# First spectral input stage: the first tile's feature transform ahead of the second tile's transposes, the second tile's fold ahead of its moments, and six dummy matmuls fewer

## Chip, cores and metric

The kernel runs on one core of one Trainium2 chip. The metric is the device time of one execution in microseconds (us). Most executions of one kernel agree within 0.3%; here that is about 2 us.

## The reference

The model alternates two residual layers, twice. The change touches the first of them only.

```python
def _A_ref(x, w_r, w_i):                     # spectral mixer, x is 1 x 2048 x 576
    X = rfft2(x)                             # over tokens and features
    X = X * (w_r + 1j * w_i)
    return irfft2(X).astype(bfloat16)
x = x + _A_ref(_layernorm(x), w_r, w_i)      # layer 1: the stage studied is its input half
x = x + _B_ref(_layernorm(x), w1, b1, w2, b2)  # MLP 576 -> 4608 -> 576
# ... the same two once more
```

## The kernel before

The 2048 tokens are 16 tiles of 128 rows. In the first spectral input stage (0 to 33 us) each tile passes through

- VectorE: `fold` (sum and difference of the row's two halves), `half_moments` and `join_moments` (variance for the layer norm);
- TensorE: `turn` (five transposes into PSUM, which ScalarE copies to `xT`), then `dft_d` (the feature transform: six matmuls of 290 columns into PSUM);
- ScalarE: a copy `z` of that result, scaled by 1/sqrt(variance). Root and reciprocal are taken for two tiles at once, so tile 0's `z` waits for tile 1's moments;
- TensorE `dft_v`, and a copy `y1` by ScalarE or VectorE in turn, which a DMA then exchanges between partitions.

Tiles are counted below in the order of processing: tile 0, 1, 2, 3. `keep_busy(n)` issues n dummy matmuls of 512 columns, whose only purpose is to keep TensorE busy.

```python
def keep_busy(n, ps=None):
    pw = (ps or sm_ps)([P, 512], F32)         # takes one of the 2 small PSUM buffers
    for _ in range(n):
        nc.tensor.matmul(pw[:], lhsT=zeros[:], rhs=zeros[:, 0:1].to_broadcast([P, 512]), start=True, stop=True)

def turn(self, t):
    xf = self.st.pop(("xf", t))
    pt = sm_ps([P, 5, P])                     # the same 2 small buffers
    # ... five transposes, then the copy by ScalarE into xT

for i in range(NT + 4):                       # run_all, cut to what matters
    if 0 <= i - 1 < NT:
        (self.turn_halves if i == NT else self.turn)(order[i - 1])
    if i < NT:
        self.fold(order[i], nc.vector)
        if i == 0:
            half_moments(0)
    if i % 2 == 0 and 2 <= i <= NT:
        inverse(i // 2 - 1)                   # reciprocal for two tiles
    if i < NT:
        join_moments(i)                       # the aggregate
    # ... dft_v(order[i - 4])
    if 0 <= i - 2 < NT:
        (self.dft_d_halves if i - 2 == NT - 1 else self.dft_d)(order[i - 2])
    if i % 2 == 1 and i < NT:
        root(i // 2)                          # ScalarE, for two tiles
    if i < 4:
        keep_busy((5, 6, 1, 1)[i])
    if i + 1 < NT:
        half_moments(i + 1)                   # moments of the next tile, ahead of its fold
    # ... loads
```

Of the kernel before, what the change touches and what calls it, by code (L numbers as in the profile page):

```python
# [19 lines left out]
NT = 16  # L20
# [108 lines left out]
def kernel(  # L129
# [28 lines left out]
    def uid():  # L158
        _n[0] += 1
        return _n[0]  # L160

    def big_ps(shape, dtype=F32):
        return ps_big.tile(shape, dtype, tag="big", name=f"psb{uid()}")
# [39 lines left out]
    order = [t for q in QUADS for t in q]  # L203
# [13 lines left out]
    def keep_busy(n, ps=None):  # L217

        pw = (ps or sm_ps)([P, 512], F32)
        for _ in range(n):  # L220
            nc.tensor.matmul(pw[:], lhsT=zeros[:], rhs=zeros[:, 0:1].to_broadcast([P, 512]), start=True, stop=True)  # L221
# [95 lines left out]
    class SpectralIn:  # L317
# [102 lines left out]
            exchange(self.vx, t, y1)  # L420

        def dft_d(self, t):
            pz = big_ps([P, 2, 512])
            if ("xT2", t) in self.st:
                xT = self.st.pop(("xT2", t))
                for o in range(2):
                    at_rest = 4 * KH + o * KP
                    nc.tensor.matmul(pz[:, o, 0:KP], lhsT=xT[:, 4, :], rhs=c_fd2[:, at_rest : at_rest + KP], start=True, stop=False)
                    for part in range(2):
                        g = FOLDS.index((o, part))  # L430
                        nc.tensor.matmul(
                            pz[:, o, part * KH : (part + 1) * KH], lhsT=xT[:, g, :], rhs=c_fd2[:, g * KH : (g + 1) * KH],
                            start=False, stop=(part == 1),
                        )
            else:
                xT = self.st.pop(("xT", t))
                for o in range(2):
                    for q, ci in enumerate(HALF_CHUNKS[o]):
                        nc.tensor.matmul(
                            pz[:, o, 0:KP], lhsT=xT[:, ci, :], rhs=c_fd[:, 3 * o + q, :], start=(q == 0), stop=(q == 2),  # L440
                        )
            z = work.tile([P, 2, KP], BF16, tag="z", bufs=3)
            nc.scalar.activation(
                out=z[:].rearrange("p r (j o) -> p r j o", o=2),
                in_=pz[:, :, 0:KP].rearrange("p o (r j) -> p r j o", r=2),
                func=ACT.Copy, scale=self.st.pop(("rs", t)),
            )
            self.st["z", t] = z
# [17 lines left out]
        def run_all(self, loads):  # L466

            stats, moments, roots = {}, {}, {}

            def half_moments(n):  # L470
                stats[n] = work.tile([P, 2, nc.vector.BN_STATS_DIM], F32, tag="ln_stats", name=f"st{uid()}")
                for h in range(2):
                    nc.vector.bn_stats(out=stats[n][:, h, :], in_=x_sb[:, order[n], h * DH : (h + 1) * DH])

            def join_moments(n):
                if n % 2 == 0:
                    moments[n // 2] = work.tile([P, 2, nc.vector.BN_AGGR_DIM], F32, tag="ln_mv", bufs=4, name=f"mv{uid()}")
                nc.vector.bn_aggr(out=moments[n // 2][:, n % 2, :], in_=stats.pop(n)[:])

            def root(m):  # L480
                roots[m] = work.tile([P, 2], F32, tag="ln_v", name=f"sq{uid()}")
                nc.scalar.activation(out=roots[m][:], in_=moments.pop(m)[:, :, 1], func=ACT.Sqrt, bias=c_eps[:, 0:1], scale=1.0)

            def inverse(m):
                rs = work.tile([P, 2], F32, tag="ln_rs", bufs=4, name=f"rs{uid()}")
                nc.vector.reciprocal(out=rs[:], in_=roots.pop(m)[:])
                for i in range(2):
                    self.st["rs", order[2 * m + i]] = rs[:, i : i + 1]

            for i in range(NT + 4):  # L490
                if 0 <= i - 1 < NT:
                    (self.turn_halves if i == NT else self.turn)(order[i - 1])
                if i < NT:
                    self.fold(order[i], nc.vector)
                    if i == 0:
                        half_moments(0)
                if i % 2 == 0 and 2 <= i <= NT:
                    inverse(i // 2 - 1)
                if i < NT:
                    join_moments(i)  # L500
                if 0 <= i - 4 < NT - 1:
                    self.dft_v(order[i - 4], on_act=(i % 2 == 0 and i < NT))
                if i - 4 == NT - 1:
                    self.dft_v_halves(order[i - 4])
                if 0 <= i - 2 < NT:
                    (self.dft_d_halves if i - 2 == NT - 1 else self.dft_d)(order[i - 2])
                if i % 2 == 1 and i < NT:
                    root(i // 2)
                if i < 4:
                    keep_busy((5, 6, 1, 1)[i])  # L510
                if i + 1 < NT:
                    half_moments(i + 1)
                for call in loads.get(i, ()):
                    call()
# [427 lines left out]
    for n, (kind, j) in enumerate(early):  # L942
        i = 1 + 5 * n // 8
# [79 lines left out]
```

## Time and profile before

| | before |
|---|---|
| time, median of 3 runs | 743.07 us (742.95 to 743.47) |
| span of the profiled run | 740.7 us |
| landing of tile 1 of x (VectorE's wait for it ends) | 5.39 us |
| reciprocal for tiles 0 and 1 | 7.78 us |
| first `z` | 8.04 us |
| end of the stage (TensorE's next 16 dummies start) | 33.05 us |

From the page of the kernel before: the busy table (engine, busy us, share of the span, number of instructions) and, under it, the shares by engine of the chain of work that ended last.

```profile
PE 728.0 (98%) x5051; PEld 455.5 (61%) x5051; DVE 272.1 (37%) x937; ACT 309.2 (42%) x530; POOL 59.9 (8%) x117
...
PE 44%; ACT 1%; DVE 0%; issue 0%; ACTq 0%
```

The chain was followed back from the end to 403 us only, hence 44% for TensorE and next to nothing for the others. It doesn't reach the stage studied here.

TensorE looks saturated. The Trainium skill warns against this reading ("Trainium Kernel Development and Optimization", "Performance Expectations": "matmul busy time (the `TensorMatrix` row) is a bad metric for how close a kernel is to roofline"). In the stretch studied part of the busy time is dummies, so one has to look at what each engine waits for.

The timeline of TensorE in the kernel before: start in us, duration in us, engine, line, operation with output<-inputs, form and count; in brackets the idle time before it and what ended that.

```profile
1.00 2.31 PE L221 MATMUL pss_122<-zeros 128*128 128x512 bf16 x5 [1.00 <-DVE h_sb L240]
3.54 0.72 PE L353 MATMUL pss_131<-ident,xf 128*128 128x128 bf16 x5 [0.23 <-DVE xf L331]
4.06 2.58 PE L221 MATMUL pss_145<-zeros 128*128 128x512 bf16 x6
6.70 0.44 PE L353 MATMUL pss_157<-ident,xf 128*128 128x128 bf16 x5
6.97 0.91 PE L439 MATMUL psb_172<-c_fd,xT 128*128 128x290 bf16 x6
7.72 0.38 PE L221 MATMUL pss_181<-zeros 128*128 128x512 bf16 x1
7.94 0.44 PE L353 MATMUL pss_188<-ident,xf 128*128 128x128 bf16 x5
...
8.97 0.38 PE L221 MATMUL pss_211<-zeros 128*128 128x512 bf16 x1
9.42 0.44 PE L353 MATMUL pss_217<-ident,xf 128*128 128x128 bf16 x5
9.70 0.66 PE L455 MATMUL psb_232<-z,c_k_82 128*128 128x290 bf16 x4
...
33.05 3.64 PE L221 MATMUL pss_713<-zeros 128*128 128x512 bf16 x16 [0.24 <-ACT shared_113 L419]
```

Rows from L221 are the dummies: 5, 6, 1 and 1; the 16 at 33.05 mark the end of the stage. The six from 4.06 end only at 6.64, 0.43 us each; the row at 7.72 takes 0.22 until the next. A row with several matmuls gives their spacing: 6 transforms from 6.97 to 7.72 are 0.125 us apart. Tile 3's transposes start at 9.42.

The timeline of VectorE in the kernel before, from the landing of tile 1 on.

```profile
5.39 0.82 DVE L473 BATCH_NORM_STATS2 st_128<-x_sb 128x6 f32<-128x288 bf16 x2 [0.71 <-DMA x_sb<-in_A_x_dram]
6.12 0.29 DVE L331 TENSOR_TENSOR xf<-x_sb 128x288 bf16<-128x288 bf16 x1
...
6.55 0.21 DVE L478 BATCH_NORM_AGGREGATE mv_120<-st_128 128x2 f32<-128x12 f32 x1
...
7.78 0.16 DVE L486 RECIPROCAL rs_168<-sq_143 128x2 f32<-128x2 f32 x1
```

And of ScalarE in the same stretch.

```profile
6.79 0.30 ACT L482 ACTIVATE sq_143<-mv_120,c_eps 128x2 f32<-128x2 f32 x1 [0.50 <-DVE mv_120 L478]
7.17 0.69 ACT L355 COPY xT<-pss_157 128x640 bf16<-128x640 bf16 x1
8.04 0.74 ACT L443 ACTIVATE z<-psb_172,rs_168 128x580 bf16<-128x580 f32 x1 [0.18 <-DVE rs_168 L486]
8.68 0.69 ACT L355 COPY xT<-pss_188 128x640 bf16<-128x640 bf16 x1
```

The first `z` (8.04) was released by VectorE's reciprocal (7.78). That stands behind everything VectorE does from 5.39 on. Behind the `z` ScalarE copies tile 2's transposes (8.68 to 9.37), and tile 3's transposes, which need that PSUM buffer, start at 9.42.

### The profile page before, as it was taken

How to read it: one execution, taken by the hardware profiler on the slowest of the kernel's cores; microseconds unless marked ns; L12 is line 12 of the kernel's file. 1: busy time of each engine (PE TensorE's matmuls, PEld its weight loads, DVE VectorE, ACT ScalarE, POOL GpSimd, SP SyncE). 2: the span in 40 equal slices, each digit the busy share in tenths (PEclk: the TensorE clock that was granted, in tenths of full speed). 3: DMA queues.
4: the chain of work that ended last, by engine and by line, in shares of the span. 5: the costliest groups of instructions: out<-in, count | busy, mean ns of one | idle time of the engine just before them, and what ended most of it. 6: DMA issues, size and time to landing. Idle time of an engine off the chain costs nothing. (4 is left out here: it accounts for less than half of the span.)

```text
span 740.7 us, 12448 instructions
## 1 busy us (share of the span) xinstructions
PE 728.0 (98%) x5051; PEld 455.5 (61%) x5051; DVE 272.1 (37%) x937; ACT 309.2 (42%) x530; POOL 59.9 (8%) x117
## 2 busy tenths in 40 slices
PE   9989999999999999999998999999999999999997
PEld 6666644774487448744875575467547744774476
DVE  7895930555045604520355778011400140020011
ACT  7776856016511561156224686620361055005600
POOL 1230002002000200000003000110100010000000
PEclk9999999999999999999999999999999999999999
DMA  9577536212112102100117401450101010100000
GB/s 300 156 181 182 191 128 194 73 52 54 36 35 53 54 15 56 45 26 1 27 45 238 120 1 65 144 160 17 45 1 44 17 45 1 44 17 9 0 18 16
DMA packets 53097, 53.81 MB, mean 73 GB/s; under 512 B 30960, under 2 KB 44528, under 8 KB 53040
## 3 DMA queue, kind: packets, MB, share of 16 engines
q1 hardware_dynamic: 45232, 27.49, 13.6%
q0 software_dynamic: 7376, 24.96, 10.6%
q8 instruction: 39, 0.64, 0.4%
q10 hardware_dynamic: 432, 0.58, 0.2%
q14 instruction: 18, 0.15, 0.1%
HBM read 28.69 MB, written 8.59 MB: 50 GB/s over the span
## 5 line engine op out<-in xcount | busy, mean ns | idle before, releaser
L859 PEld LDWEIGHTS <-h_sb 128*128 128x128 bf16 x2304 | 224.9, 98 | 58.5 <-issue 1.0
L813 PEld LDWEIGHTS <-w_sb 128*128 128x128 bf16 x1152 | 109.4, 98 | 142.4 <-issue 17.2
L769 DVE TENSOR_SCALAR xn<-x_sb,mv,rs 128x576 bf16<-128x576 bf16 x24 | 9.4, 427 | 67.1 <-DMA quad_1809<-xn 28.8
L288 DVE BATCH_NORM_STATS2 stats<-x_sb 128x6 f32<-128x288 bf16 x78 | 30.9, 438 | 0.0
L821 PEld LDWEIGHTS <-w1r_sb 64*128 64x128 bf16 x288 | 10.8, 94 | 24.5 <-issue 16.9
L855 DVE TENSOR_TENSOR xb<-x_sb,b_bc 128x576 f32<-128x576 bf16 x32 | 24.0, 749 | 0.0
L569 PEld LDWEIGHTS <-h_sb 128*128 128x128 bf16 x128 | 12.1, 97 | 11.7 <-issue 5.2
L772 POOL COPY xn<-xn 128x64 bf16<-128x64 bf16 x24 | 6.4, 266 | 150.9 <-DVE xn L769 150.9
L221 PEld LDWEIGHTS <-zeros 128*128 128x128 bf16 x108 | 10.8, 102 | 11.5 <-issue 2.8
L827 ACT ACTIVATE h_sb<-psb_6037,b_sb 128x512 bf16<-128x512 f32 x2 | 1.3, 684 | 37.9 <-PE psb_6037 L821 37.9
L827 ACT ACTIVATE h_sb<-psb_6635,b_sb 128x512 bf16<-128x512 f32 x2 | 1.3, 684 | 37.8 <-PE psb_6635 L821 37.8
L827 ACT ACTIVATE h_sb<-psb_7233,b_sb 128x512 bf16<-128x512 f32 x2 | 1.3, 684 | 37.8 <-PE psb_7233 L821 37.8
L538 PEld LDWEIGHTS <-c_f_83 128*128 128x128 bf16 x128 | 12.3, 97 | 7.6 <-issue 3.0
L882 DVE TENSOR_TENSOR x_sb<-psb_7473,xb 128x576 bf16<-128x576 f32 x1 | 0.8, 758 | 43.4 <-PE psb_7473 L859 43.4
L882 DVE TENSOR_TENSOR x_sb<-psb_4089,xb 128x576 bf16<-128x576 f32 x1 | 0.8, 758 | 39.5 <-PE psb_4089 L859 39.5
L369 DVE TENSOR_TENSOR xf<-ef 128x256 bf16<-128x256 f32 (+1 forms) x56 | 13.6, 306 | 0.5
L882 DVE TENSOR_TENSOR x_sb<-psb_6875,xb 128x576 bf16<-128x576 f32 x1 | 0.8, 759 | 33.6 <-PE psb_6875 L859 33.6
L882 DVE TENSOR_TENSOR x_sb<-psb_6277,xb 128x576 bf16<-128x576 f32 x1 | 0.8, 758 | 33.6 <-PE psb_6277 L859 33.6
L455 PEld LDWEIGHTS <-c_k_82 128*128 128x128 bf16 x120 | 11.2, 98 | 2.5
L882 DVE TENSOR_TENSOR x_sb<-psb_3285,xb 128x576 bf16<-128x576 f32 x1 | 0.8, 757 | 28.8 <-PE psb_3285 L859 28.8
L882 DVE TENSOR_TENSOR x_sb<-psb_2483,xb 128x576 bf16<-128x576 f32 x1 | 0.8, 758 | 28.7 <-PE psb_2483 L859 28.7
L727 ACT ACTIVATE h_sb<-x_sb 128x576 bf16<-128x576 bf16 x16 | 11.2, 699 | 0.1
(1397 smaller groups left out, 1522.9 us busy)
## 6 DMA issues: line engine op xcount, KB each, us to landing
w_sb<-in_B_w_dram SPq DMA_DIRECT2D x16, 288.0 KB
v_sb<-in_B_w_dram POOLq DMA_DIRECT2D x4, 1152.0 KB, 6.0
shared_1504<-in_B_w_dram POOLq DMA_DIRECT2D x2, 1440.0 KB, 7.5
shared_5434<-in_B_w_dram POOLq DMA_DIRECT2D x2, 1440.0 KB, 7.5
v_sb<-shared_4685 SPq DMA_DIRECT2D x16, 145.0 KB
out_dram<-x_sb SPq DMA_DIRECT2D x15, 144.0 KB
v_sb<-shared_113 POOLq DMA_DIRECT2D x13, 145.0 KB, 3.4
b_sb<-shared_712 POOLq DMA_DIRECT2D x13, 145.0 KB, 6.6
```

Source lines behind the costliest of these rows:

```text
L221: nc.tensor.matmul(pw[:], lhsT=zeros[:], rhs=zeros[:, 0:1].to_broadcast([P, 512]), start=True, stop=True)
L288: nc.vector.bn_stats(out=stats[:, h, :], in_=x_sb[:, t, h * DH : (h + 1) * DH])
L369: nc.vector.tensor_tensor(out=xf[:, at0 : at0 + 2 * n].rearrange("p (g d) -> p g d", g=2), in0=ef[:, :, first : first + n], in1=ef[:, :, b ...
L455: nc.tensor.matmul(py[:, r, 0:KP], lhsT=c_k1[:, pl, :], rhs=z[:, ri], start=(q == 0), stop=(q == 1))
L538: nc.tensor.matmul(px[:, o, 0:KP], lhsT=c_f2[:, n // 4, pl, n % 4, :], rhs=vx[:, e, ri, :], start=(q == 0), stop=(q == 1))
L569: nc.tensor.matmul((ph, odd)[o][:, o, 0:KP], lhsT=i1[:, pl, n % 4, :], rhs=xp[:, ri, :], start=(q == 0), stop=(q == 1))
L727: nc.scalar.activation(out=at(h_sb, [P, D], 512 * 34), in_=x_sb[:, self.quad[i], :], func=(ACT.Copy, ACT.Square)[k], accum_out=self.s12[:, ...
L769: nc.vector.tensor_scalar(out=xn[:, 0:D], in0=x_sb[:, self.quad[i], :], scalar1=mean, scalar2=rs, op0=ALU.subtract, op1=ALU.mult)
L813: nc.tensor.matmul(acc[p][q], lhsT=w1_sb[:, ci, fc * 128 : (fc + 1) * 128], rhs=yT[:, ci, :], start=(first and ci == 0), stop=(not first a ...
L821: nc.tensor.matmul(acc[p][q], lhsT=w1r_sb[rows, p, :], rhs=yT[rows, 4, :], start=first, stop=not first)
L855: nc.vector.tensor_tensor(out=xb[:], in0=xr, in1=b2_bc[:].rearrange("p (h n) -> p h n", h=2), op=ALU.add)
L859: nc.tensor.matmul(po[:, h, 0:DH], lhsT=hts[fc][:, i * 128 : (i + 1) * 128], rhs=w2_chunk(fc)[:, h * DH : (h + 1) * DH], start=(fc == 0), ...
```

## The change

The intent is to fill TensorE's early time with real work instead of dummies. The transform of tile 0 goes ahead of tile 1's transposes, split from its scaled copy, which cannot run yet; six of the 13 dummies go; and tile 1's fold goes ahead of its moments, so that its transposes are fed sooner.

```diff
         def dft_d(self, t):
+            self.dft_d_sum(t)
+            self.dft_d_copy(t)
+
+        def dft_d_sum(self, t):
             pz = big_ps([P, 2, 512])
+            self.st["pz", t] = pz
# ... the matmuls
+        def dft_d_copy(self, t):
+            pz = self.st.pop(("pz", t))
# ... the scaled copy z
                     self.fold(order[i], nc.vector)
-                    if i == 0:
-                        half_moments(0)
+                    if i < 2:
+                        half_moments(i)
# ...
-                if 0 <= i - 2 < NT:
-                    (self.dft_d_halves if i - 2 == NT - 1 else self.dft_d)(order[i - 2])
+                if i == 1:
+                    keep_busy(2)
+                    self.dft_d_sum(order[0])
+                elif 0 <= i - 2 < NT:
+                    (self.dft_d_copy if i == 2 else self.dft_d_halves if i - 2 == NT - 1 else self.dft_d)(order[i - 2])
                 if i % 2 == 1 and i < NT:
                     root(i // 2)
-                if i < 4:
-                    keep_busy((5, 6, 1, 1)[i])
-                if i + 1 < NT:
+                if i == 0:
+                    keep_busy(5)
+                if 2 <= i + 1 < NT:
                     half_moments(i + 1)
```

## The prediction

> **What bounds the kernel.** TensorE is busy 98% of the 740.7 us span (busy table); the chain that ended last is nearly all TensorE. The change touches only the first 10 us of the first spectral stage (0 to 33 us). There the timeline shows TensorE running 13 dummy matmuls (5 from 1.00, 6 from 4.06, 1 at 7.72, 1 at 8.97). VectorE's chain sets the start: the second tile of x lands at 5.39 us (a 0.71 us wait for the DMA), then moments 5.39, fold 6.12, aggregate 6.55, moments and fold of tile 2, reciprocal 7.78; that releases ScalarE's first scaled copy z at 8.04. From 9.42 to 17 us TensorE is packed (1.52 us a tile); from 12.6 to 28 us VectorE is packed (3.18 us per two tiles). So the stage's end follows VectorE's early chain and the transposes of tile 3.
>
> **What the change does.**
> - Removes 6 of 13 dummies; nothing waits for them.
> - Tile 1's fold is ready about 0.73 us earlier (its moments move behind it), near 5.9. Its transposes queue behind the feature transform of tile 0.
> - That transform moves from 6.97 to about 5.1-5.6: it needs the first xT (copied by 4.99) and the transform constants, whose queue moves its last packets at 5.0 to 5.6. It probably runs at the slow clock. The Trainium skill ("TensorE: Matmul & The Clock Gate", Part 1) gives N/1.2 ns per matmul cold; the early dummies agree (0.43 us apart). Estimate for 6 matmuls of 290 columns: 1.45 us instead of 0.75, ending near 6.6-7.0. Tile 1's transposes then end near 6.9-7.5, against 7.14.
> - VectorE does the same work before the same reciprocal, but the aggregate now directly follows its own moments, which costs about 0.12 us (moments to aggregate is 0.85 for tile 0; with the fold between, 0.73 + 0.42).
> - z of tile 0 still waits for root and reciprocal, so it starts at 8.05 to 8.2; the advanced transform's result just waits in PSUM. The expected gain is off the critical path.
> - With fewer dummy tiles the small PSUM buffers alternate sooner. Before, tile 3's transposes (9.42) waited for the copy of tile 2 (ending 9.37) in their buffer, though the fold was ready at 9.15. Now they follow the fold, about 9.35: 0.06 us back, and 0.2 us of VectorE slack at 11.7 absorbs its 0.12.
>
> **Critical path.** Stage: about -0.1 to +0.15 us; later stages shift with it. The risk is the clock: TensorE gets gaps near 4.9-5.4, 7.0-7.9 and 8.9-9.3 that dummies filled. The same part of the skill says the array turns fast after a busy window of about 3.4 us, whose phase is free-running. In before it is fast from 6.70. If it turns later, tiles 1 to 3 run at half speed and 0.5 to 2 us are lost; about one chance in six.
>
> **Predicted time: 743.0 us, range 742.3 to 744.2.** Faster by over 2%: 0.3%; within 2%: 99%; slower: 0.7%.
>
> **What would show it.** Right: first z at 8.05-8.2, just behind the reciprocal; transform of tile 0 at 5.1-5.6, matmuls about 0.24 us apart; stage end (last y1 copies, 33.4 before) within 0.2 us; the rest shifted equally. Wrong: first z before 7.9, the stage's end moved by over 0.4 us, or the transform of tile 1 still slow (1.45 us, not 0.75).
>
> **What would make it wrong.** A later change to the fast clock; constants landing after 5.8 us, which would hold tile 1's transposes behind the waiting transform; a different landing of x; or load and exchange traffic shifting the 0.5 us wait for exchanged data at 37.2 us.

## The result

The changed kernel took 743.50 us (median of 6 runs, 742.36 to 743.84); the kernel before took 743.01 us in the rounds counted with it (6 runs, 742.67 to 743.50). The ratio is 1.0002, with a 95% interval of 0.9989 to 1.0015. A ratio is the mean time of one kernel's runs over that of the other's of the same rounds, so it is not quite the ratio of the medians.

From the page of the changed kernel, the busy table:

```profile
PE 726.3 (98%) x5045; PEld 454.5 (61%) x5045; DVE 272.1 (37%) x937; ACT 308.8 (42%) x530; POOL 59.9 (8%) x117
```

TensorE does 1.7 us less (728.0 to 726.3) and the span is 740.9 instead of 740.7: the busy time that went was worth nothing.

The timeline of TensorE in the changed kernel:

```profile
3.58 0.72 PE L353 MATMUL pss_128<-ident,xf 128*128 128x128 bf16 x5 [0.26 <-DVE xf L331]
4.09 1.06 PE L221 MATMUL pss_143<-zeros 128*128 128x512 bf16 x2
5.46 0.91 PE L444 MATMUL psb_146<-c_fd,xT 128*128 128x290 bf16 x6 [0.31 <-DMA c_fd<-const_fd]
6.21 0.44 PE L353 MATMUL pss_160<-ident,xf 128*128 128x128 bf16 x5
8.11 0.56 PE L353 MATMUL pss_182<-ident,xf 128*128 128x128 bf16 x5 [1.46 <-DVE xf L331]
...
9.40 0.56 PE L353 MATMUL pss_209<-ident,xf 128*128 128x128 bf16 x5
9.79 0.66 PE L463 MATMUL psb_224<-z,c_k_82 128*128 128x290 bf16 x4
...
33.18 3.64 PE L221 MATMUL pss_705<-zeros 128*128 128x512 bf16 x16 [0.24 <-ACT shared_113 L419]
```

The transform of tile 0 now runs at 5.46 instead of 6.97 (after a wait of 0.31 for its constants), tile 1's transposes at 6.21 instead of 6.70. Then TensorE waits 1.46 us for the fold of tile 2. Tile 3's transposes start at 9.40, nearly where they did before (9.42).

The timeline of VectorE in the changed kernel:

```profile
5.65 0.31 DVE L331 TENSOR_TENSOR xf<-x_sb 128x288 bf16<-128x288 bf16 x1 [0.94 <-DMA x_sb<-in_A_x_dram]
...
6.10 0.81 DVE L481 BATCH_NORM_STATS2 st_139<-x_sb 128x6 f32<-128x288 bf16 x2
6.95 0.21 DVE L486 BATCH_NORM_AGGREGATE mv_120<-st_139 128x2 f32<-128x12 f32 x1
...
8.18 0.16 DVE L494 RECIPROCAL rs_171<-sq_153 128x2 f32<-128x2 f32 x1
...
9.05 0.29 DVE L331 TENSOR_TENSOR xf<-x_sb 128x288 bf16<-128x288 bf16 x1
```

And of ScalarE:

```profile
7.19 0.29 ACT L490 ACTIVATE sq_153<-mv_120,c_eps 128x2 f32<-128x2 f32 x1 [0.86 <-DVE mv_120 L486]
...
8.38 0.74 ACT L451 ACTIVATE z<-psb_146,rs_171 128x580 bf16<-128x580 f32 x1 [0.31 <-DVE rs_171 L494]
```

In this profile tile 1 of x landed at 5.65, 0.26 us later than in the profile of before. Counted from that landing the reciprocal comes 8.18 - 5.65 = 2.53 us later (before: 7.78 - 5.39 = 2.39), and the first `z`, issued right behind it, starts at 8.38 although its input had been in PSUM since about 6.4 (5.46 + 0.91). The stage ended at 33.18 (before 33.05), which is 27.53 us after the landing (before 27.66).

So the quantity to compare is the length from tile 1's landing, which takes the chance of the load out. A second mark helps: the row of TensorE that follows tile 3's transposes (9.70 in the kernel before, 9.79 in the changed one). From it to the stage's end the profiles take between 23.3 and 23.6 us (the kernel without dummies apart), so what a variant gains or loses is nearly all decided by then. All lengths in us:

| kernel | landing of tile 1 | landing to reciprocal | landing to the end of tile 3's transposes | from there to the stage's end | landing to the stage's end | full clock from |
|---|---|---|---|---|---|---|
| before | 5.39 | 2.39 | 4.31 | 23.35 | 27.66 | 6.3 |
| changed | 5.65 | 2.53 | 4.14 | 23.39 | 27.53 | 5.2 |
| changed, again | 5.39 | 2.53 | 4.14 | 23.36 | 27.50 | 7.3 |
| only the fold | 5.31 | 2.53 | 4.43 | 23.36 | 27.79 | 4.6 |
| only the transform | 5.38 | 2.39 | 3.99 | 23.39 | 27.38 | 6.3 |
| gap filled | 5.23 | 2.53 | 4.14 | 23.38 | 27.52 | 4.6 |
| two dummies fewer | 5.64 | 2.39 | 4.00 | 23.53 | 27.53 | 7.5 |
| own root | 5.43 | - | 4.83 | 23.49 | 28.32 | 9.6 |
| own root, filled | 5.09 | - | 4.41 | 23.34 | 27.75 | 4.7 |
| no dummies | 5.31 | 2.53 | 4.95 | 23.93 | 28.88 | 11.4 |
| before, second group later | 5.49 | 2.39 | 4.30 | 23.35 | 27.65 | 4.3 |
| combined | 5.41 | 2.39 | 4.00 | 23.48 | 27.48 | 7.1 |

The last column is the moment, from the span's start, at which the trace records TensorE's clock as granted in full. It agrees with the spacing of the matmuls: dummies are 0.43 us apart before it and 0.22 after it. (A text below gives 9.8 for the first own-root kernel; the record has 9.6.) The two kernels with moved constants are missing because there tile 1 is no longer the tile whose load holds up the reciprocal.

Each length comes from one profile. The two profiles of the changed kernel differ by 0.03 us, and the kernel with the later second group, which leaves this path as it was, by 0.01 us from the kernel before.

The second mark is not the only one that fits. From 8.4 to 28.8 us TensorE, VectorE and ScalarE of the changed kernel are busy for 20.32, 20.35 and 20.40 of 20.40 us, so each of them can carry a delay on. The start of ScalarE's second `z` (tile 1) is the tighter mark. From it to the stage's end all kernels take 23.77 to 23.79 us where tile 3's transposes wait for the copy of tile 2 (the kernel before, only the fold, and the kernel before with either load moved), and all others 23.55 to 23.59, but for the combined kernel (23.64) and the one without dummies (24.22). ScalarE as a second carrier of the delay was not tested by a run of its own.

### The profile page after: what moved, and what is told of

The parts are those of the page before. It is cut to its first block, busy times and chain, and to the rows that moved or that the text cites. A ratio compares the mean times of both kernels' runs of the same rounds, so it can differ in the third digit from the quotient of the medians.

```text
span 740.9 us, 12435 instructions
## 1 busy us (share of the span) xinstructions
PE 726.3 (98%) x5045; PEld 454.5 (61%) x5045; DVE 272.1 (37%) x937; ACT 308.8 (42%) x530; POOL 59.9 (8%) x117
## 5 line engine op out<-in xcount | busy, mean ns | idle before, releaser
L444 PEld LDWEIGHTS <-xT 128*128 128x128 bf16 x96 | 9.3, 97 | 4.2 <-issue 0.9
```

Of the source, the lines that this page charges most:

```text
L444: nc.tensor.matmul(pz[:, o, 0:KP], lhsT=xT[:, ci, :], rhs=c_fd[:, 3 * o + q, :], start=(q == 0), stop=(q == 2),)
```

## The experiments

Theory A, as predicted: VectorE's chain from the landing of tile 1 to the transposes of tile 3 sets the stage's length. The transform's early place is off that path; the fold's early place costs the chain 0.12 to 0.14 us; the removed dummies free a small PSUM buffer, which gives about as much back. Theory B: the missing dummies make the clock turn late in some runs, which would explain why the first six times of the changed kernel fall into two groups (742.4-742.6 and 743.2-743.8). Theory C: tile 1 lands later because of the change. Theory D: the early transform is itself worth time. Theory E, named in two of the texts: the dummies matter only through the clock. Every kernel was timed in 5 rounds against the kernel before, and all gave correct results.

### The changed kernel again

No edit. What was expected:

> The changed kernel once more, unaltered, to get its distribution and a second profile. Theory A (nothing on the critical path changed; the spread of 742.4 to 743.8 us seen so far is chance of each run): median within 0.4 us of the kernel before in the same rounds, spread of about 1.5 us again, and in the profile the reciprocal of tile 0 about 2.53 us after the landing of the second tile of x (before: 2.39). Theory B (without the dummies the array turns to its fast clock later in some runs, which makes the slow group at 743.8): two groups of times 1.2 us apart, the kernel before without the upper group; and a profile that falls in the upper group shows first transforms at 0.24 us a matmul. Rival C (the second tile of x lands later in the changed kernel, 5.65 against 5.39 us, for a reason that belongs to the change): it lands at 5.6 or later again.

Median 743.24 us (741.97 to 743.55, 5 runs) against 743.00 (742.51 to 744.34, 9 runs), ratio 0.9998 (0.9985 to 1.0010). The two groups did not come back, and the kernel before spread wider than the changed one. Tile 1 landed at 5.39, so theory C falls. The reciprocal came 2.53 us after it, as in the first profile. This time the clock turned late, at 7.3. TensorE's timeline of this run:

```profile
5.18 1.61 PE L444 MATMUL psb<-c_fd,xT 128*128 128x290 bf16 x6
6.58 0.74 PE L353 MATMUL pss<-ident,xf 128*128 128x128 bf16 x5
...
8.24 0.91 PE L444 MATMUL psb<-c_fd,xT 128*128 128x290 bf16 x6
```

The six transforms of tile 0 take until 6.58, 0.23 us apart, and those of tile 1 (8.24) are fast. Yet the stage took 27.50 us, against 27.53 with the clock full from 5.2 on. A turn as late as 7.3 costs this kernel nothing, because TensorE still waits 0.52 us for VectorE's fold of tile 2, until 7.84.

### Each half alone, and the gap filled

Only the fold (the kernel before, plus):

```diff
-                    if i == 0:
-                        half_moments(0)
+                    if i < 2:
+                        half_moments(i)
# ...
-                if i + 1 < NT:
+                if 2 <= i + 1 < NT:
                     half_moments(i + 1)
```

> Only the VectorE half of the change: the fold of the second tile ahead of its moments; TensorE keeps the order and the 13 dummies of before. Theory A: aggregate of the second tile 1.30 us after its landing instead of 1.16, reciprocal and first z 0.13 us later relative to that landing, stage end unchanged within 0.2 us after allowing for the landing; time within 0.3 us of before. If the earlier fold were worth something by itself: first z earlier, time 0.3 to 0.7 us lower.

Only the transform and the seven dummies: the changed kernel with those lines taken back.

> Only the TensorE half: transform of the first tile ahead of the second tile's transposes and 7 dummies, while the moments stay ahead of the fold. Theory A: reciprocal 2.39 us after the landing of the second tile as before, first z right behind it, time within 0.3 us of before. Theory B: the same double grouping of times as the full change (it has the same gaps in TensorE), some runs 1 us slow.

Four dummies in TensorE's gap (the changed kernel, plus):

```diff
+                if i == 2:
+                    pz = self.st["pz", order[1]] = big_ps([P, 2, 512])   # the bank the next transform overwrites
+                    for _ in range(4):
+                        nc.tensor.matmul(pz[:, 0, :], lhsT=zeros[:], rhs=zeros[:, 0:1].to_broadcast([P, 512]), start=True, stop=True)
```

> The full change with 4 dummies of 512 columns put back into TensorE's 1.5 us gap ahead of the third tile's transposes, written into the bank that the next transform overwrites, so that no buffer is added. Theory A: time equal to the changed kernel within 0.3 us. Theory B: the upper group vanishes and the median falls to that of the changed kernel's lower group, about 742.4 to 742.7.

The times resolve nothing: medians 742.82, 742.98 and 743.00 us, each with a ratio of 0.9996 to before and an interval of about ±0.0013. The lengths in the table do. Against the kernel before, the fold alone makes the stage 0.13 us longer (27.79 against 27.66), the transform half alone makes it 0.28 shorter (27.38), and both together 0.13 to 0.16 shorter (27.53, 27.50): the sum of the two. All of it is there by the end of tile 3's transposes (+0.12, -0.32 and -0.17 against 4.31); from there on the three kernels take the same 23.36 to 23.39 us. Filling the gap changes nothing (27.52), and its times (742.02 to 743.17) are spread like those of the repeated changed kernel (741.97 to 743.55). Theory B falls for the changed kernel as it is.

The fold's cost is in the order of VectorE's rows. With the fold between moments and aggregate, the aggregate starts 6.55 - 5.39 = 1.16 us after the landing. With the aggregate right behind its own moments it starts 6.95 - 5.65 = 1.30 us after it: it has to wait for their result (from 6.10 to 6.95, that is 0.85, where the fold starts 0.73 behind the moments in the kernel before).

### Two dummies fewer

What gains 0.28 us in the transform half: the transform, or the buffers? The kernel before, with only its last two single dummies left out:

```diff
-                if i < 4:
-                    keep_busy((5, 6, 1, 1)[i])
+                if i < 2:
+                    keep_busy((5, 6)[i])
```

> The kernel before with only the two single dummies behind tiles 1 and 2 left out (13 become 11), so that the small PSUM buffers alternate as in the changed kernel; transform and fold stay where they were. Theory A' (the TensorE half of the change gains only because the dummies' tiles no longer take every second small buffer, so tile 3's transposes follow the fold instead of the copy of tile 2): the time from the landing of the second tile of x to the end of the stage falls from 27.66 to 27.4 us (the transform-only kernel: 27.38), tile 3's transposes start about 3.6 us after that landing (transform-only: 3.59, before: 4.03). Rival D (the transform's early place gains it): the stage stays at 27.6 to 27.7. The whole time is within 0.4 us of before either way.

Median 743.49 us (742.38 to 743.65) against 743.08 (742.28 to 743.93), ratio 1.0003 (0.9990 to 1.0015). TensorE's timeline:

```profile
6.94 0.67 PE L353 MATMUL pss<-ident,xf 128*128 128x128 bf16 x5
...
9.24 0.56 PE L353 MATMUL pss<-ident,xf 128*128 128x128 bf16 x5
9.64 0.66 PE L455 MATMUL psb<-z,c_k 128*128 128x290 bf16 x4
```

Tile 3's transposes start 9.24 - 5.64 = 3.60 us after the landing, as in the transform-only kernel (8.97 - 5.38 = 3.59), where the kernel before has 4.03. They end 4.00 us after it (transform-only 3.99, before 4.31). So up to there the whole gain comes from the buffers, and rival D falls for this part. Each `keep_busy` took one of the two small PSUM buffers, so that all the early transposes shared the other: this is what tied tile 3's transposes to ScalarE's copy of tile 2 and, through it, to the first `z`.

At the stage's end only half of that is left (27.53, between 27.66 and 27.38). In this run the clock turned only at 7.5 and tile 1's transposes (6.94) were slow; ScalarE's first `z` came 2.76 us after the landing, where the transform-only kernel has 2.58. That `z` (8.40) starts right behind the end of tile 0's transform (7.43 + 0.93 = 8.36), which stands behind the slow transposes here. The combined kernel below has the transform early and a clock that turned nearly as late (7.1), and its first `z` comes at 2.58. So the last 0.15 us seems to need both, the late clock and the transform in its old place: with a late clock the early transform may be worth that much. No run tests this by itself.

### The loads

The transform constants issued behind the first two tiles of x, in both kernels:

```diff
     for t in QUADS[0]:
         nc.sync.dma_start(out=x_sb[:, t, :], in_=xv[:, t, :])
-    nc.scalar.dma_start(out=c_fd[:], in_=const_ap("fd"))
-    nc.scalar.dma_start(out=c_k1[:], in_=const_ap("k1"))
+        if t == QUADS[0][1]:
+            nc.sync.dma_start(out=c_fd[:], in_=const_ap("fd"))
+    nc.sync.dma_start(out=c_k1[:], in_=const_ap("k1"))
```

> The kernel before with the loads of the transform constants issued behind the first two tiles of x, on the same queue. Theory A (the stage is paced by VectorE's chain from the landing of the second tile of x): that tile lands 0.3 to 0.8 us sooner than 5.39, the reciprocal comes 2.39 us behind it and the stage ends earlier by as much as it landed earlier, at 32.3 to 32.7 us. If something else bounds the stage (TensorE, the loads), its end stays at 32.9 to 33.2. The whole time at most 0.7 us lower, since the wait for exchanged data ahead of the second layer's middle (0.3 to 1.3 us in the profiles so far) may take it back.

> The changed kernel with the same reordering of loads. Now the transform that was brought ahead waits for its constants: its start moves from 5.2-5.5 to about 5.8-6.3 us and tile 1's transposes wait behind it. Theory A: as tile 1's transposes have until the first z, 2.7 us after the landing, minus 0.6 for their copy, the stage still ends 27.5 us after the landing of the second tile of x, or up to 0.4 us later if the constants land later than 6.3. Rival D (early transform valuable): it loses what it gained, the stage ends 28 us or more after the landing.

The kernel before with this order: 743.74 us (742.56 to 743.83), ratio 1.0004 (0.9991 to 1.0016). VectorE's timeline shows why it did not gain:

```profile
5.69 0.20 DVE L479 BATCH_NORM_AGGREGATE mv<-st 128x2 f32<-128x12 f32 x1
6.85 0.82 DVE L474 BATCH_NORM_STATS2 st<-x_sb 128x6 f32<-128x288 bf16 x2 [0.95 <-DMA x_sb<-in_A_x_dram]
...
8.01 0.16 DVE L487 RECIPROCAL rs<-sq 128x2 f32<-128x2 f32 x1
```

Tile 1 now lands before VectorE is free to take it (its aggregate is at 5.69 instead of 6.55), but then VectorE waits 0.95 us for tile 2, which stands behind the constants. The reciprocal comes at 8.01 and the stage ends at 33.25, 25.24 us behind it (before: 33.05 - 7.78 = 25.27). The expectation that the stage would end sooner failed, because the wait moved one tile on. That the end follows the reciprocal by the same distance fits theory A.

In the changed kernel the order does harm: 744.01 us (742.75 to 744.63), ratio 1.0010 (0.9997 to 1.0022), which is not clear of "same". TensorE's timeline of its profile:

```profile
6.23 1.61 PE L445 MATMUL psb<-c_fd,xT 128*128 128x290 bf16 x6 [1.19 <-DMA c_fd<-const_fd]
7.63 1.27 PE L354 MATMUL pss<-ident,xf 128*128 128x128 bf16 x10
9.16 1.03 PE L445 MATMUL psb<-c_fd,xT 128*128 128x290 bf16 x6 [0.25 <-ACT xT L356]
```

The transform waits 1.19 us for its constants with tile 1's transposes behind it, and in this run the clock turns full only at 9.4. The first `z` starts at 9.00 and the stage ends at 33.78. The early transform makes the kernel depend on the landing of the constants, where the kernel before had slack. The expectation of theory A failed. By its letter rival D's outcome came in: tile 1's fold starts without a wait at 4.52, so the stage ends at least 33.78 - 4.52 = 29.26 us after that landing. But the wait of VectorE had moved to tile 2 here as well (moments at 6.59), and the late clock is mixed in, so this run doesn't show that the early place is worth time.

The second group of x (576 KB) issued behind the first `xT` instead of at once:

```diff
-    load_x(1)
# ...
-    paced = {}
+    paced = {1: [lambda: load_x(1, ("turn", order[0]))]}
```

> The kernel before with the load of the second group of x (576 KB) issued behind the first xT instead of at once, so that the second tile of x shares the queues with less. Theory A (the stage is paced by VectorE's chain from the second tile of x): that tile lands at 4.7 to 5.2 us instead of 5.23 to 5.65, reciprocal 2.39 us behind it, first copy of y1 on VectorE 6.5 us behind it, end of the stage 0.2 to 0.5 us earlier than 33.05. If the third tile is late instead (as when the constants were moved), the reciprocal waits for it and nothing is gained. The second group must land by 9.2 us; if it does not, the stage gets longer by the difference. Whole time within 0.5 us of before.

Tile 1 landed at 5.49, so the premise was wrong: that load was not what held it up. Instead VectorE waited 0.39 us for the later group at 9.8 us, without consequence: the stage took 27.65 us (before 27.66). The time was 743.71 us (743.23 to 744.64), ratio 1.0005 (0.9993 to 1.0017).

### Letting the early transform be used

If `z` did not wait for tile 1, would the early transform pay? A root and a reciprocal for tile 0 alone:

```diff
+            def root_one(i):      # ScalarE, one column of the pair
+            def inverse_one(i):   # VectorE, one column
# ...
+                if i == 0:
+                    root_one(0)
+                if i == 1:
+                    inverse_one(0)
+                    self.dft_d_copy(order[0])
+                    root_one(1)
+                if i == 2:
+                    inverse_one(1)
```

> The changed kernel with a root and a reciprocal of tile 0's own, so that the first z does not wait for the second tile's moments: the result of the early transform is used as soon as it is there. Theory A (z was not what bounds the stage; VectorE's fold of tile 3 and after it TensorE are): the first z starts near 7.0 us instead of 8.1-8.4, and the stage still ends 27.4 to 27.6 us after the landing. Rival D (the early transform is worth something once z follows it): the stage shortens by 0.4 us or more, to 27.1 or less.

743.40 us (742.57 to 744.03), ratio 1.0004 (0.9991 to 1.0018). The first `z` came at 7.37, but the stage took 28.32 us. The run is confounded. ScalarE now waits for the first root ahead of its first copy, TensorE idles 0.52 us for `xT`, the clock turns full only at 9.6, and tile 1's root waits behind the `z`. So it was mended: both roots ahead of the first `z` and behind the first copy, one dummy more ahead of the transform, and the four dummies of above in the gap.

> The own root for tile 0 again, with ScalarE's order mended (both roots ahead of the first z, first copy not delayed) and TensorE kept busy by five more dummies. Theory A: fast clock before 8 us; first z near 7.1 to 7.3 us, about 1 us sooner than 8.11-8.38; VectorE's first copy of y1 still 6.4 to 6.6 us and the stage end still 27.5 to 27.7 us behind the landing of the second tile. Rival D (early z is worth something): 6.1 or less and 27.1 or less. Theory E (the slow clock until 9.8 us was what lengthened the first own-root kernel, whose stage took 28.3 us): the length falls back to 27.5-27.7 with the clock.

743.29 us (742.52 to 744.39), ratio 1.0001 (0.9988 to 1.0013). The clock was full from 4.7. ScalarE's first `z`:

```profile
6.93 0.74 ACT L452 ACTIVATE z<-psb,rs 128x580 bf16<-128x580 f32 x1
```

That is 6.93 - 5.09 = 1.84 us after the landing, where the changed kernel has 8.38 - 5.65 = 2.73. The stage took 27.75 us, 0.22 longer than in the changed kernel and a little outside what theory A expected (27.5 to 27.7). The second reciprocal has become later by the first one ahead of it and that one's wait for its root, 7.89 - 5.09 = 2.80 us after the landing instead of 2.53, and tile 3's transposes end 0.27 later with it (4.41 against 4.14). From there to the stage's end it takes the usual 23.34 us. So a first `z` 0.9 us sooner gains at most 0.05 us here, and a VectorE chain 0.27 us later costs about as much as it is late: theory D falls in this kernel, and the two numbers fit theory A. Between the two own-root kernels the stage fell by 0.57 us; clock and order changed together, so the split is open.

### No dummies

The changed kernel without any of its seven dummies:

```diff
-                    keep_busy(2)
                     self.dft_d_sum(order[0])
# ...
-                if i == 0:
-                    keep_busy(5)
```

> The changed kernel without any of its seven dummies. Theory E (dummies matter only through the clock: a busy stretch is needed): the array turns fast at 8 us or later, transforms of tiles 0 and 1 run at 0.24 us a matmul, the stage ends 28.2 us or more behind the landing of the second tile, and the whole time is 0.5 to 1.5 us above before. If the dummies are worth nothing, the stage takes 27.5 us as in the changed kernel.

TensorE's timeline of its profile, then VectorE's row for its first copy of `y1`, the result of `dft_v`:

```profile
5.12 1.61 PE L444 MATMUL psb<-c_fd,xT 128*128 128x290 bf16 x6 [0.85 <-DMA c_fd<-const_fd]
...
8.27 1.66 PE L444 MATMUL psb<-c_fd,xT 128*128 128x290 bf16 x6
```

```profile
13.05 0.76 DVE L470 CAST shared<-psb 128x580 bf16<-128x580 f32 x1 [0.63 <-PE psb L463]
```

Both transforms run slowly, 0.23 to 0.24 us apart. The clock is full only from 11.4 us, VectorE now waits for TensorE (0.63 us), and the stage takes 28.88 us, 1.35 longer than in the changed kernel. This profile's run took 746.18 us; the six runs span 742.35 to 746.18 with a median of 743.97, against 743.47 for before, ratio 1.0007 (0.9993 to 1.0022), so the cost in the mean is not clear. In the profile, at least, the dummies are worth 1.35 us, and what shows in it is the late clock.

### The parts that the runs point to, together

The transform half, moments ahead of the fold, four dummies in the gap, the second group of x later; the edits are those shown above.

> The parts that the runs point to, together: transform ahead of the second tile's transposes and seven dummies as in the changed kernel, moments ahead of the fold as before, four dummies in TensorE's gap, and the second group of x later. Theory A: reciprocal 2.39 us and VectorE's first copy of y1 6.32 us behind the landing of the second tile, stage end 27.4 us behind it, so at about 32.2 to 32.6 us if that tile lands at 4.8 to 5.2. Whole time at most 0.7 us below before; not clear of the spread of single runs.

742.44 us (742.38 to 742.83, 5 runs) against 743.47 (742.59 to 744.34, 11 runs), ratio 0.9988 with an interval of 0.9976 to 1.0000. This is the best median, but the interval reaches 1, and its profile does not show where 0.9 us would come from: tile 1 landed at 5.41 (not at 4.8 to 5.2, as hoped), the stage took 27.48 us, and the span is 740.7, that of the kernel before. It is not shown to be faster. The texts also expected VectorE's first copy of `y1` at 6.3 to 6.6 us behind the landing; in the three kernels whose texts name it (second group later, own root filled, combined) it came at 6.73 to 6.84, and the stage's end did not follow (27.65 with 6.84).

### Where a gain in the stage goes afterwards

The transform-only kernel ended its stage 0.29 us sooner than before (32.76 against 33.05), but its profiled span is 741.4 against 740.7. TensorE's timeline at the start of the second layer's middle part, in the kernel before and then in the transform-only kernel:

```profile
394.97 3.64 PE L221 MATMUL pss_4686<-zeros 128*128 128x512 bf16 x16 [0.24 <-ACT y_361_4663 L419]
398.73 0.66 PE L538 MATMUL psb_4703<-b_sb,c_f_83 128*128 128x290 bf16 x4
```

```profile
394.33 3.64 PE L221 MATMUL pss<-zeros 128*128 128x512 bf16 x16 [0.24 <-ACT y L419]
399.03 2.64 PE L549 MATMUL psb<-b_sb,c_f 128*128 128x290 bf16 x20 [1.06 <-DMA b_sb<-y]
```

At 394 us the transform-only kernel is still 0.64 us ahead. Then it waits 1.06 us for exchanged data and starts 0.30 us behind. The kernel before had no such wait in its profile; among the others it goes from none to 1.5 us. Between 384 and 405 us the queues carry 4.4 MB, mostly weight loads for that stage. What decides the length of this wait from run to run was not tested; it is larger than anything that the change does.

## Why the prediction was right

- **Time and range.** Predicted 743.0 us, 742.3 to 744.2; measured 743.50. This says little by itself: single runs of the kernel before spread from 742.28 to 744.34. What tests the mechanism are the lengths.
- **First `z` behind the reciprocal.** Right: in both profiles of the changed kernel it starts 0.19 to 0.20 us behind it. It came at 8.38 in the first (outside 8.05-8.2, since tile 1 landed 0.26 us later) and at 8.11 in the second. The early transform's result waited in PSUM, as said, and the own-root kernels show that taking it sooner gains nothing.
- **The fold costs VectorE about 0.12 us.** Measured 0.14, in every kernel that has it with the shared root.
- **Buffers give it back.** Right in kind and sign, too small in size. Predicted were 0.06 us at tile 3's transposes; measured are 0.17 at their end and 0.13 to 0.16 at the stage's end, counted from the landing, a little outside the predicted -0.1 to +0.15. The transposes start on the first half of the fold (9.05 to 9.34 in the changed kernel), not on the whole of it as the prediction assumed. Two dummies fewer reproduce the effect without the rest of the change.
- **The slow clock for the transform.** Estimated at 1.45 us. The result's profile shows it fast (0.75 until the next row, clock full from 5.2); the repeat shows it slow (1.40). This term depends on the run, and neither case moved the stage. With the fast one, tile 1's transposes ended at 6.65 instead of the 6.9 to 7.5 expected.
- **The clock as the risk.** Of two profiles of the changed kernel none turned late enough to matter. The loss is real where TensorE idles longer: the kernels with late constants, with the own root and without dummies turned at 9.4 to 11.4 and their stages ended 0.7 to 1.1 us later than before.
- **"Later stages shift with it."** This step failed. The changed kernel was 0.13 us behind at 33 us and 0.12 us ahead at 394.9 us; in the second layer a wait for exchanged data re-draws the difference. It is not the wait that the prediction named: that one, at 37.2 us, stayed (0.49 before, 0.52 changed). The forecast held because both shifts are small, not because the shift was carried; to that extent it was luck.

## What to carry to other kernels

Bringing an instruction forward pays only if its consumer was waiting for it: here the consumer waited for a reciprocal, and the gain that the runs explain came from a side effect, dummies that no longer took every second PSUM buffer. Dummies that only hold the clock should write where they take no buffer from real work, and they are worth keeping as long as an idle stretch could delay the full clock. When single times spread over 2 us, measure a change of 0.1 us as a length inside the trace, from the event that releases the stage to its end.

## What the Trainium skill lacked or had wrong

- "TensorE: Matmul & The Clock Gate", Part 1, says that the clock turns full after a busy window of about 3.4 us with a free-running phase. The runs agree: with the gaps filled, or nearly, it turned between 4.3 and 7.5 us, a spread of 3.2. The page does not say how much idle time such a window may hold. As an estimate from the page's 3.4 us, the window that ends with the turn at 9.4 of the changed kernel with moved constants reaches back to 6.0 and holds about 0.47 us of idle time (0.22 until 6.23, and 0.25 ahead of 9.16), and it still turned the clock. Where the limit lies these runs do not show.
- The same page, Part 4, says that transposes do not engage the full clock. Here five transposes took 0.52 us to the next row early (3.54 to 4.06 in the kernel before) and 0.27 once the clock was full (6.70 to 6.97): they run at the full clock when other work has turned it.
- "ScalarE: Activation LUTs", "What ACT_TABLE_LOAD costs", gives 1283 ns for the load and about 1380 ns of drain, 2.66 us for a switch. The load agrees (1283 ns in the own-root trace); the drain does not show. ScalarE's timeline of the changed kernel with moved constants has the copy ending at 4.92, the load at 4.94 and the root at 6.24, 1.32 us in all:

```profile
4.23 0.69 ACT L356 COPY xT<-pss 128x640 bf16<-128x640 bf16 x1 [1.81 <-PE pss L354]
4.94 1.28 ACT L491 ACT_TABLE_LOAD   x1
6.24 0.29 ACT L491 ACTIVATE sq<-mv,c_eps 128x2 f32<-128x2 f32 x1
```

- "VectorE: DVE Perf Modes", "The DRAIN you can't avoid", gives no cost for an instruction that reads its predecessor's result. Here an aggregate starts 0.85 us after its two moments instructions start, where an independent fold starts 0.73 after them: about 0.12 us.
